# An attention and FFN kernel with its 483 work units queued in another order

## The chip, the cores and the metric

The kernel runs on one core of one Trainium2 chip. The metric is device time in microseconds (us), the median of several runs. A core has five engines that run side by side, each with its own in-order queue: TensorE (PE) multiplies matrices and reads its stationary operand in a separate weight load (PEld), VectorE (DVE) and ScalarE (ACT) work element by element and empty PSUM, the accumulator memory that only TensorE writes, GpSimd (POOL) does casts and small copies between SBUF tiles, and SyncE (SP) issues transfers, which 16 DMA engines carry out. An instruction waits at the head of its queue until the semaphores it needs have been counted up; everything behind it on that engine waits as well.

## The reference

The computation is an attention with a sparse mask, followed by a feed-forward block (FFN) whose hidden layer is the maximum of three products:

```python
scores = scale * np.matmul(q, k.transpose(0, 1, 3, 2))       # 4 batches, 8 heads, 768 rows, width 64
keep = is_global | is_local                                  # the first 8 keys, and the last 96
scores = np.where(keep, scores + bias, -1e9)                 # bias = -slope[head] * distance
a = np.exp(scores - max); a = a / (sum(a) + 1e-9)
x = np.matmul(a, v)                                          # brought to (3072, 512)
h = np.maximum(np.maximum(x @ w1, x @ w2), x @ w3)           # 512 -> 768
out = h @ w_out                                              # 768 -> 512
```

Inputs and output are float32. The kernel casts to bf16 on the chip.

## The kernel before

The 3072 rows are 24 tiles of 128 rows, six to a batch (tiles 0 to 5 are batch 0). For the FFN the tiles are gathered in seven chunks of 4, 2, 2, 4, 4, 4 and 4 tiles, so chunk 0 holds tiles 0 to 3, chunk 1 tiles 4 and 5, chunk 2 tiles 6 and 7, chunk 3 tiles 8 to 11, and so on. A tile needs keys of itself and of the tile before; the eight global keys are put over the first eight columns of a tile's transposed keys, where only later tiles read them.

The whole kernel is a list of units, written out by hand or by a planner as the string `SCHEDULE` (lines 25 to 57). The last lines of the kernel go through it in order, and each unit puts its instructions at the end of the queues of its engines. The scheduling is manual, so the order on every engine, SP's transfers among them, is the order of the string. The first letter names the unit, the numbers that follow its tile or part, and often as the last number the engine that does the copy (0 ACT, 1 DVE, 2 POOL, other values other ways):

- `l` (line 151) loads a part of q or k for a group of tiles: l0, l1, l2 are tiles 0 and 1, 2 and 3, 4 and 5 (q and k, 512 KB each), l3 is tiles 6 to 9 (four parts), l4 tiles 10 and 11. `c` (178) casts such a part to bf16, `x` (226) transposes it with eight matmuls into PSUM and copies the result out.
- `L` (160) loads q and k of one tile from tile 12 on, `C` with 0 (185) casts them, `X` (245) transposes them: with a last number 4 as one DMA transposition on SP, otherwise with eight matmuls and copies.
- `v` loads v of a tile (256 KB), `C` with 1 casts it. `V` and `G` copy the global rows and columns.
- `w` loads weights (w0.0 to w0.2 of 512 KB, w1.0 to w1.2 of 1024 KB), `W` casts a third of them: W0 serves the hidden blocks f = 0 and 1, W1 those of 2 and 3, W2 those of 4 and 5. `o` and `Q` do the same for the output weights. `K` and `B` make the masks.
- `S` (268) computes the scores of one tile and one half of the heads into PSUM (buffers sp0 or sp1) and takes the exponential on ACT. With a last number 1 the mask is added by two more matmuls, otherwise `M` (302) multiplies it on DVE.
- `A` (311) multiplies the probabilities with v into the same two PSUM buffers and normalises on DVE (rz, xb). `T` (335) transposes the result into `xT` of its chunk: by four matmuls and a copy, or with a last number 4 by one DMA transposition on SP.
- `F` (355) computes one of the three products of a chunk and hidden block: F0.4.1 is chunk 0, block 4, second product. ACT copies the first, DVE takes the maximum with the second and third. `O` (385) multiplies a tile's hidden layer with the output weights and stores it; `E` does so for the last chunk. `D` (432) is a few matmuls on zeros.

F, O, part of `x`, `X` and the first four `T` share three PSUM buffers, `psH`. The loads of q and k share five buffers, the loads of v six.

Of the kernel before, what the change touches and what calls it, by code (L numbers as in the profile page):

```python
# [22 lines left out]


SCHEDULE = """
    K0 K1 K2 K3 K4 K5 l1.0 l1.1 D0.3 c0.0.2 B0.1 B1.1 B2.1 B3.0 K6 B4.1 B5.1 c0.1.1 c1.0.2 x0.0.4 B6.1
    B7.1 x0.1.4 S0.0.1 v0 l2.0 l2.1 K7 S0.1.1 G0.0 S1.0.1 S1.1.0 x1.0.3 c1.1.2 M0.0 M0.1 M1.0 v1 x1.1.4
    C0.1.2 v2 A0.1 G1.2 S2.0.1 M1.1 c2.0.2 x2.0.1 C1.1.1 S2.1.0 G2.2 S3.0.1 M2.0 M2.1 C2.1.1 T0.1 S3.1.1
    M3.0 M3.1 c2.1.2 v3 A1.0 C3.1.0 w0.0 V1.2 x2.1.2 w1.0 A2.1 V2.2 A3.0 T1.0 T2.1 T3.1 W1.0.1 W0.0.0
    G3.2 S4.0.0 S4.1.0 F0.0.0 F0.1.0 M4.0 F0.2.0 F0.3.0 G4.1 S5.0.0 M4.1 S5.1.0 w0.1 W0.1.1 w0.2 W0.2.2  # L30
    V3.2 F0.0.1 F0.1.1 F0.0.2 F0.1.2 v4 C4.1.0 A4.0 V4.2 w1.1 W1.1.2 W2.0.0 F0.4.0 F0.5.0 M5.0 M5.1 w1.2
    W1.2.2 v5 W2.1.0 T4.0 F0.2.1 F0.3.1 l3.0 l3.2 F0.4.1 l3.1 c3.0.2 c3.2.2 F0.5.1 o2 C5.1.0 A5.1 l3.3
    F0.2.2 Q2.2 F0.3.2 W2.2.0 o0 T5.0 F0.4.2 o1 F0.5.2 x3.0.0 F1.0.0 F1.1.0 c3.1.1 F1.2.0 x3.2.0 Q0.2
    F1.0.1 F1.1.1 F1.2.1 l4.0 l4.1 c3.3.0 F1.0.2 F1.1.2 F1.2.2 x3.1.2 x3.3.1 F1.3.0 F1.4.0 Q1.2 F1.3.1
    S6.0.0 S6.1.0 v6 v7 v8 G6.0 F1.3.2 F1.5.0 v9 c4.0.1 F1.4.1 S7.0.0 S7.1.0 G7.2 v10 M6.0 M6.1 M7.0
    M7.1 O0.0.0 F1.4.2 c4.1.1 C6.1.2 C7.1.2 L12 F1.5.1 S8.0.0 S8.1.0 x4.0.0 O0.1.0 A6.0 x4.1.2 A7.1 V7.2
    F1.5.2 v11 T6.0 O0.2.0 T7.1 G8.2 C8.1.2 S9.0.0 S9.1.0 G9.1 v12 v13 O0.3.0 F2.0.0 F2.1.0 S10.0.0 M8.0
    M8.1 M9.0 M9.1 S10.1.0 C9.1.2 L13 L14 F2.0.1 F2.1.1 F2.0.2 A8.0 C12.0.1 F2.1.2 G10.2 O1.0.0 V8.2
    A9.1 X12.1 M10.0 M10.1 C10.1.0 C11.1.0 F2.2.0 S11.0.0 S11.1.0 M11.0 M11.1 L15 F2.3.0 F2.4.0 O1.1.0
    V9.2 A10.1 F2.2.1 V10.2 T8.0 F2.3.1 F2.5.0 T9.0 A11.1 F2.4.1 T10.0 F2.2.2 F2.3.2 T11.1 F2.4.2  # L40
    S12.0.0 S12.1.0 F2.5.1 C13.0.2 C14.0.2 C15.0.1 X13.4 F3.0.0 F3.1.0 F3.0.1 G12.1 C12.1.0 F3.2.0
    F3.1.1 F3.2.1 S13.0.0 S13.1.0 F2.5.2 v14 C13.1.0 C14.1.2 M12.0 M12.1 F3.0.2 F3.1.2 X14.4 F3.2.2
    X15.4 G13.2 M13.0 M13.1 S14.0.0 S14.1.0 F3.3.0 F3.4.0 F3.5.0 M14.0 M14.1 G14.1 A12.0 A13.1 F3.3.1
    F3.4.1 F3.5.1 S15.0.0 M15.0 S15.1.0 G15.0 v15 V13.2 L16 L17 v16 T12.4 v17 M15.1 O2.0.0 C15.1.0 A14.0
    V14.2 F3.3.2 F3.4.2 T13.4 F3.5.2 C16.1.0 C16.0.2 X16.3 T14.4 C17.0.2 A15.1 X17.4 O2.1.0 S16.0.0
    S16.1.0 G16.1 L18 V15.2 L19 T15.1 M16.0 O3.0.0 M16.1 F4.0.0 F4.1.0 F4.0.1 F4.1.1 C18.0.2 L20 C19.0.2
    A16.1 F4.2.0 F4.3.0 S17.0.0 S17.1.0 F4.2.1 F4.0.2 F4.3.1 v18 M17.0 v19 M17.1 X18.3 X19.4 C20.0.0
    V16.2 F4.1.2 C17.1.2 O3.1.1 A17.1 F4.2.2 F4.3.2 S18.0.0 M18.0 S18.1.0 M18.1 F4.4.0 T16.4 T17.4
    F4.4.1 C18.1.2 C19.1.1 F4.4.2 X20.4 G18.1 S19.0.0 S19.1.0 F4.5.0 L21 M19.0 M19.1 v20 F4.5.1 A18.0
    T18.4 F4.5.2 A19.1 T19.4 V19.1 C21.0.1 X21.4 G19.1 L22 C22.0.2 L23 X22.4 O3.2.1 O3.3.0 O4.0.1  # L50
    S20.0.0 S20.1.0 M20.0 G20.0 O4.1.0 F5.0.0 F5.1.0 F5.2.0 S21.0.0 S21.1.0 G21.2 F5.0.1 F5.1.1 M20.1
    M21.0 F5.3.0 F5.0.2 F5.1.2 F5.2.1 F5.2.2 v21 C20.1.1 C21.1.2 F5.4.0 S22.0.0 M21.1 S22.1.0 C23.0.0
    F5.3.1 M22.0 M22.1 F5.5.0 F5.3.2 A20.0 V20.2 G22.2 v22 F5.4.1 X23.4 v23 F5.5.1 T20.4 A21.1 V21.1
    T21.4 F5.4.2 F5.5.2 S23.0.0 S23.1.0 M23.0 O4.2.0 M23.1 C22.1.2 A22.0 C23.1.0 O4.3.0 V22.2 T22.4
    A23.1 T23.4 O5.0.1 O5.1.0 O5.2.1 O5.3.0 F6.0.0 F6.1.0 F6.0.1 F6.0.2 F6.2.0 F6.3.0 F6.4.0 F6.1.1
    F6.2.1 F6.1.2 F6.3.1 F6.4.1 F6.2.2 F6.3.2 F6.5.0 F6.4.2 F6.5.1 F6.5.2 E
"""


# [1 line left out]
def kernel(  # L61
# [272 lines left out]

    def u_XT(T, how):
        c, i = where[T]
        if i == 0:
            xT[c] = xT_pool.tile([128, NP, len(chunks[c]) * 128], BF16, name="xT", tag="xT")
        if how == 4:
            nc.sync.dma_start_transpose(out=xT[c][:, :, i * 128:(i + 1) * 128],  # L340
                                        in_=xb[T].rearrange("p h d -> p (h d)"))
            return
        if early(T):
            tp = psH.tile([128, NP, 128], BF16, name="xtp", tag="h")
        else:
            tp = psT.tile([128, NP, 128], BF16, name="xtp", tag="tp")
        x = xb[T].rearrange("p h d -> p (h d)")
        for jp in range(NP):
            nc.tensor.transpose(tp[:, jp], x[:, jp * 128:(jp + 1) * 128], identb)  # L349
# [4 lines left out]

    def u_F1(c, f, j):
        W = len(chunks[c]) * 128
        if f == 0 and j == 0:
            ht[c] = ht_pool.tile([128, NF, W], BF16, name="ht", tag="ht")
        ps = psH.tile([128, W], FP32, name="h", tag="h")
        for dm in range(4):  # L360
            nc.tensor.matmul(ps, w123[f // 2][:, dm, j, (f % 2) * 128:(f % 2) * 128 + 128],  # L361
                             xT[c][:, dm], start=(dm == 0), stop=(dm == 3))
# [147 lines left out]
```

## Time and profile before

| | |
|---|---|
| Median of 3 runs | 180.03 us (179.93 to 180.16) |
| Span of the profiled execution | 178.3 us |
| TensorE busy | 166.9 us, 94% |
| VectorE, ScalarE, GpSimd busy | 118.9, 103.1, 37.5 us |
| DMA moved | 35.52 MB, 83587 packets |
| DMA transpositions on SP | 11 of results (`xT<-xb`), 9 of q/k pairs (`qkT<-qkb`) |

The span is what the profiler saw from the first to the last instruction; the run time is a little longer. In the profile, a row of digits gives the busy share in 40 slices of the span (9 is 90% or more). The chain is the work that ended last, followed back step by step to what released each instruction. A row of a timeline gives start, duration, engine, line, operation, output and input, the number of instructions and, in brackets, how long the engine had been idle and what ended that. Matmul durations overlap, so what a unit costs TensorE is read from the distance of starts.

### The profile page before, as it was taken

The page shows a single profiled execution, that of the slowest core. Times are in us where ns is not written, and L with a number is a line of the kernel's source. Part 1 is how long each engine was busy: PE and PEld are TensorE (multiplying, and loading weights), DVE is VectorE, ACT ScalarE, POOL GpSimd, SP SyncE. Part 2 cuts the span into 40 slices and gives each one's busy share as a digit, 9 for nine tenths or more (in the row PEclk, how much of TensorE's full clock was granted, in tenths as well). Part 3 has the DMA queues.
Part 4 walks back from the last instruction along what each step waited for, and adds up shares of the span by engine and source line. Part 5 has one row for each costly group of instructions (what it writes and reads, how often), then busy time and mean ns, then how long its engine had stood idle before and what let it go on. Part 6 is the DMA issues. An engine that isn't in the chain of part 4 may idle for free.

```text
span 178.3 us, 3960 instructions
## 1 busy us (share of the span) xinstructions
PE 166.9 (94%) x1529; PEld 95.8 (54%) x1551; DVE 118.9 (67%) x237; ACT 103.1 (58%) x160; POOL 37.5 (21%) x65
## 2 busy tenths in 40 slices
PE   3599799999999999999999999999999999999992
...
DMA  5999999999998999989544999769889674610006
GB/s 140 292 271 242 357 320 384 320 361 358 251 193 213 229 254 236 174 171 233 94 90 118 159 247 235 157 132 186 173 153 294 136 143 146 224 42 4 0 11 226
DMA packets 83587, 35.52 MB, mean 199 GB/s; under 512 B 66160, under 2 KB 78320, under 8 KB 83568
## 3 DMA queue, kind: packets, MB, share of 16 engines
...
## 4 chain that ended last, share of the span: by engine, by line
PE 85%; DMA 8%; SPq 2%; issue 1%; POOL 1%; DVE 1%; ACT 1%; ACTq 0%
PE h L361 53%; PE po L376 17%; PE sp L283 6%; DMA rawv<-in_v_dram 4%; DMA rawp<-in_q_dram 4%; PE op L322 3%; PE op L325 2%; SPq L174 2%; PE tpp L239 2%; PE xtp L349 1%; SPq L158 1%; POOL qkp L183 1%; PE tp L261 1%; DVE xb L332 0%; ACT va L189 0%
## 5 line engine op out<-in xcount | busy, mean ns | idle before, releaser
L361 PE MATMUL h<-xT,w 128*128 128x512 bf16 (+1 forms) x491 | 99.2, 348 | 0.7 <-issue 0.2
L361 PEld LDWEIGHTS <-w 128*128 128x128 bf16 x504 | 46.9, 98 | 40.5 <-DVE w L427 0.3
L288 ACT ACTIVATE P<-sp 128x1024 bf16<-128x1024 f32 (+1 forms) x48 | 43.4, 955 | 20.6 <-PE sp L283 20.4
L368 DVE TENSOR_TENSOR h<-h,h 128x512 bf16<-128x512 bf16 (+1 forms) x42 | 25.3, 610 | 25.7 <-PE h L361 16.5
L366 ACT CAST h<-h 128x512 bf16<-128x512 f32 (+1 forms) x42 | 21.6, 533 | 21.5 <-PE h L361 21.3
L376 PE MATMUL po<-wo,ht 128*128 128x512 bf16 (+2 forms) x147 | 33.1, 362 | 0.5
L370 DVE TENSOR_TENSOR ht<-h,h 128x512 bf16<-128x512 bf16 (+1 forms) x42 | 25.1, 607 | 3.7 <-PE h L361 3.0
L307 DVE TENSOR_TENSOR P<-P,wmask 128x1024 bf16<-128x1024 bf16 x36 | 24.8, 718 | 3.6 <-ACT P L288 3.5
L376 PEld LDWEIGHTS <-ht 128*128 128x128 bf16 x156 | 14.0, 98 | 13.9
L382 ACT COPY ost<-po 128x512 f32<-128x512 f32 (+2 forms) x20 | 11.2, 564 | 17.8 <-PE po L376 17.7
L332 DVE TENSOR_TENSOR xb<-op,rz 128x512 bf16<-128x512 f32 x24 | 16.6, 692 | 0.8
L283 PEld LDWEIGHTS <-qkT 64*128 64x128 bf16 x352 | 10.2, 96 | 10.0 <-issue 8.0
L283 PE MATMUL sp<-qkT 64*128 64x128 bf16 x352 | 15.2, 223 | 0.4 <-DVE xb L332 0.4
L322 PEld LDWEIGHTS <-P 128*128 128x128 bf16 x192 | 12.5, 97 | 2.5 <-ACT P L288 0.2
L221 POOL COPY va<-vaf 8x260 int32<-8x260 int32 x14 | 6.3, 452 | 34.5 <-PE op L325 34.5
L198 POOL CAST qkb<-raw 128x1024 bf16<-128x1024 f32 x7 | 7.2, 1037 | 27.7 <-DMA raw<-in_q_dram 18.9
L322 PE MATMUL op<-va,P 128*128 128x65 bf16 x160 | 12.3, 193 | 0.7 <-ACT va L189 0.6
L239 PE MATMUL tpp<-identb,qkp 128*128 128x128 bf16 x96 | 8.5, 246 | 4.0 <-POOL qkp L183 3.4
L325 PEld LDWEIGHTS <-P 128*128 128x128 bf16 x160 | 10.4, 97 | 2.2 <-issue 0.7
L239 PEld LDWEIGHTS <-qkp 128*128 128x128 bf16 x96 | 7.0, 111 | 5.8 <-POOL qkp L183 4.3
L325 PE MATMUL op<-va,P 128*128 128x65 bf16 x128 | 9.9, 193 | 0.0
L243 ACT COPY qkT<-tpp 128x1024 bf16<-128x1024 bf16 (+1 forms) x9 | 7.9, 874 | 3.4 <-PE tpp L239 3.4
...
## 6 DMA issues: line engine op xcount, KB each, us to landing
...
```

What stands on the lines that cost most here:

```text
L239: nc.tensor.transpose(tp[:, e, j - lo], qb["p", n, s][:, e, 2 * j:2 * j + 2].rearrange("i h d -> i (h d)"), identb)
L283: nc.tensor.matmul(sp[:, hh, j2, ds], qT(T - ds, 1)[hsl, jp], qT(T, 0)[hsl, jp], start=not how, stop=True, skip_group_check=True)
L288: nc.scalar.activation(P[:, :, 0:n], sp.rearrange("p a b d n -> p (a b) d n")[:, :, 0:n], AF.Exp, bias=0.0, scale=scale)
L307: nc.vector.tensor_mul(P, P, wmask[:, g, :, 0:2])
L322: nc.tensor.matmul(o, P[:, i, 0], heads(va[T])[:, h], start=True, stop=(t == 0), skip_group_check=True)
L325: nc.tensor.matmul(o, P[:, i, 1], heads(va[T - 1])[:, h], start=False, stop=True, skip_group_check=True)
L332: nc.vector.tensor_tensor(out=x.rearrange("p (g h) d -> p g h d", g=2), in0=o4[:, :, :, 0:64], in1=rz[:, :, :, None].to_broadcast([128, 2, ...
L361: nc.tensor.matmul(ps, w123[f // 2][:, dm, j, (f % 2) * 128:(f % 2) * 128 + 128], xT[c][:, dm], start=(dm == 0), stop=(dm == 3))
L366: nc.scalar.copy(h01, ps)
L368: nc.vector.tensor_max(h01s[c, f], h01s[c, f], ps)
L370: nc.vector.tensor_max(ht[c][:, f], h01s[c, f], ps)
L376: nc.tensor.matmul(po, ht[c][:, f, tt * 128:(tt + 1) * 128], wo[:, f, cols], start=(f == 0), stop=(f == NF - 1))
```

## The change

The same 483 units stand in another order. The order alone moves three kinds of things:

- The attention of tiles 0 to 5 up to its scores stands ahead of the first FFN unit, with `A4`, `T4`, `A5` and `T5` between the first FFN units of chunk 0; in the order before, S4 stands ahead of the first FFN unit and S5 behind it. In the opening, part x3.0 of tiles 6 to 9 also comes ahead of the FFN, the four l3 loads stand among the weight loads instead of behind them, and `D0.3` stands behind x0.0 instead of first. From there on, FFN units of chunks 0, 1 and 2 are interleaved more finely.
- X16 and X18 go from matmuls to a DMA transposition (11 by DMA instead of 9), and T8, T9 and T10 as well (14 by DMA instead of 11).
- Seventy-odd units have another engine for their copy, cast or PSUM buffer. On the whole POOL gets casts of w and v from ACT and DVE. Six score units have their mask from matmuls, as before, but partly others (S1.1, S4.0, S4.1, S5.1 in the place of S1.0, S2.0, S3.0, S3.1).

Two lines of code allow for an order in which the first unit of a chunk is not always the same: the tile is made by whichever unit comes first. The diff, with the string cut to what is spoken of:

```diff
-    K0 K1 K2 K3 K4 K5 l1.0 l1.1 D0.3 c0.0.2 B0.1 B1.1 B2.1 B3.0 K6 B4.1 B5.1 c0.1.1 c1.0.2 x0.0.4 B6.1
-    B7.1 x0.1.4 S0.0.1 v0 l2.0 l2.1 K7 S0.1.1 G0.0 S1.0.1 S1.1.0 x1.0.3 c1.1.2 M0.0 M0.1 M1.0 v1 x1.1.4
-    C0.1.2 v2 A0.1 G1.2 S2.0.1 M1.1 c2.0.2 x2.0.1 C1.1.1 S2.1.0 G2.2 S3.0.1 M2.0 M2.1 C2.1.1 T0.1 S3.1.1
-    M3.0 M3.1 c2.1.2 v3 A1.0 C3.1.0 w0.0 V1.2 x2.1.2 w1.0 A2.1 V2.2 A3.0 T1.0 T2.1 T3.1 W1.0.1 W0.0.0
-    G3.2 S4.0.0 S4.1.0 F0.0.0 F0.1.0 M4.0 F0.2.0 F0.3.0 G4.1 S5.0.0 M4.1 S5.1.0 w0.1 W0.1.1 w0.2 W0.2.2
-    V3.2 F0.0.1 F0.1.1 F0.0.2 F0.1.2 v4 C4.1.0 A4.0 V4.2 w1.1 W1.1.2 W2.0.0 F0.4.0 F0.5.0 M5.0 M5.1 w1.2
-    W1.2.2 v5 W2.1.0 T4.0 F0.2.1 F0.3.1 l3.0 l3.2 F0.4.1 l3.1 c3.0.2 c3.2.2 F0.5.1 o2 C5.1.0 A5.1 l3.3
-    F0.2.2 Q2.2 F0.3.2 W2.2.0 o0 T5.0 F0.4.2 o1 F0.5.2 x3.0.0 F1.0.0 F1.1.0 c3.1.1 F1.2.0 x3.2.0 Q0.2
-    F1.0.1 F1.1.1 F1.2.1 l4.0 l4.1 c3.3.0 F1.0.2 F1.1.2 F1.2.2 x3.1.2 x3.3.1 F1.3.0 F1.4.0 Q1.2 F1.3.1
-    S6.0.0 S6.1.0 v6 v7 v8 G6.0 F1.3.2 F1.5.0 v9 c4.0.1 F1.4.1 S7.0.0 S7.1.0 G7.2 v10 M6.0 M6.1 M7.0
-    M7.1 O0.0.0 F1.4.2 c4.1.1 C6.1.2 C7.1.2 L12 F1.5.1 S8.0.0 S8.1.0 x4.0.0 O0.1.0 A6.0 x4.1.2 A7.1 V7.2
...
-    A9.1 X12.1 M10.0 M10.1 C10.1.0 C11.1.0 F2.2.0 S11.0.0 S11.1.0 M11.0 M11.1 L15 F2.3.0 F2.4.0 O1.1.0
-    V9.2 A10.1 F2.2.1 V10.2 T8.0 F2.3.1 F2.5.0 T9.0 A11.1 F2.4.1 T10.0 F2.2.2 F2.3.2 T11.1 F2.4.2
...
+    K2 B3.1 c0.1.1 K7 B4.1 B1.2 B7.2 c0.0.0 K0 K6 K3 B0.1 B2.1 B6.1 x0.0.4 D0.3 x0.1.4 K4 B5.1 K5
+    l1.0 c1.0.2 l1.1 v1 c1.1.2 K1 S0.0.1 S1.1.1 M1.1 S1.0.0 C1.1.2 G0.2 G1.2 x1.0.3 M0.0 x1.1.4 M1.0
+    S0.1.1 S2.0.0 S2.1.0 v0 C0.1.1 A1.0 l2.1 c2.1.2 V1.0 G2.2 l2.0 c2.0.2 M2.1 M2.0 S3.0.0 S3.1.0
+    l3.0 x2.1.1 M3.1 T1.0 x2.0.2 G3.1 M0.1 A0.0 S4.1.1 v2 v3 M3.0 C2.1.2 c3.0.2 A2.0 V2.0 x3.0.2
+    C3.1.2 A3.1 S4.0.1 G4.1 M4.0 T2.1 T0.0 w0.0 W0.0.2 T3.1 S5.1.1 S5.0.0 M5.0 v4 v5 w0.1 F0.1.0
+    l3.3 V3.2 F0.0.0 M4.1 C4.1.2 A4.1 V4.0 c3.3.0 W0.1.2 C5.1.2 F0.1.1 F0.0.1 w0.2 W0.2.2 w1.0 M5.1
+    A5.1 T4.1 x3.3.2 F0.1.2 W2.0.2 T5.0 F0.0.2 F1.1.0 F1.1.1 F1.1.2 W1.0.1 l3.1 l3.2 F0.5.0 c3.2.1
+    c3.1.2 x3.1.2 F0.3.0 x3.2.4 F0.2.0 G6.0 S7.1.0 S7.0.0 F1.2.0 w1.1 W1.1.1 F0.3.1 W2.1.2 F0.5.1
+    S6.0.0 S6.1.0 M6.1 F1.2.1 F0.2.1 w1.2 W1.2.2 v7 G7.0 S8.1.0 l4.1 c4.1.2 S8.0.0 M7.0 F0.3.2 M6.0
+    F0.2.2 M7.1 F0.4.0 F1.4.0 v6 C6.1.2 F1.2.2 W2.2.2 A6.1 C7.1.2 G8.2 F1.5.0 x4.1.0 F0.5.2 A7.0 L12
+    o2 Q2.2 F1.3.0 l4.0 o0 o1 v8 v9 Q0.2 T6.1 M8.0 v12 F1.5.1 F1.5.2 c4.0.0 S9.0.0 S9.1.0 G9.0
+    F1.3.1 F1.3.2 F1.4.1 T7.1 L13 v10 C12.0.3 F0.4.1 F2.2.0 M9.1 V7.2 x4.0.0 C9.1.1 F1.0.0 F2.2.1
+    F0.4.2 S10.1.0 L15 L14 S10.0.0 G10.0 X12.1 Q1.2 O0.3.1 O0.2.0 v13 M10.1 M8.1 O0.0.0 M9.0 F1.4.2
+    v14 C8.1.2 A8.0 V8.2 v11 C10.1.2 M10.0 F2.4.0 F1.0.1 F1.0.2 S11.0.0 S11.1.0 O0.1.0 A9.0 V9.2
+    T8.4 C13.0.2 X13.4 F2.5.0 M11.0 F2.4.1 C15.0.2 F2.4.2 S12.0.0 S12.1.0 T9.4 F2.5.1 F2.5.2 M12.0
+    A10.0 F2.3.0 T10.4 C14.0.2 M11.1 V10.2 F2.0.0 X14.4 F2.2.2 C11.1.1 L16 X15.4 v16 C13.1.1 O1.0.1
+    F2.3.1 A11.0 O1.1.0 M12.1 F2.0.1 G12.0 F2.1.0 F2.1.1 T11.1 S13.0.0 L19 v15 L18 S13.1.0 F2.0.2
+    G13.1 F2.3.2 M13.0 F2.1.2 F3.2.0 S14.0.0 S14.1.0 L17 F3.4.0 F3.4.1 O2.1.1 C12.1.2 A12.0 T12.4
+    F3.4.2 F3.3.0 M14.1 F3.0.0 F3.0.1 C14.1.0 M13.1 G14.1 F3.5.0 C19.0.0 M14.0 F3.2.1 A13.1 V13.2
+    F3.2.2 C16.0.2 X16.4 T13.4 F3.5.1 S15.0.0 M15.0 C18.0.0 S15.1.0 C15.1.2 F3.5.2 M15.1 X19.4
...
+    A16.1 L21 L20 v19 F4.4.1 S19.0.0 v23 v20 L22 v21 S18.1.0 F4.5.1 F4.3.0 S17.1.0 S18.0.0 M19.0
...
+    A23.1 F5.5.0 F5.5.1 F5.5.2 T23.4 O5.2.1 O5.3.1 F6.0.0 F6.0.1 F6.3.0 F6.4.0 F6.5.0 F6.4.1 F6.5.1
+    F6.4.2 F6.1.0 O5.1.0 F6.0.2 F6.3.1 F6.2.0 F6.1.1 F6.2.1 O5.0.0 F6.2.2 F6.3.2 F6.1.2 F6.5.2 E
```

```diff
     def u_XT(T, how):
         c, i = where[T]
-        if i == 0:
+        if c not in xT:
             xT[c] = xT_pool.tile([128, NP, len(chunks[c]) * 128], BF16, name="xT", tag="xT")
...
     def u_F1(c, f, j):
         W = len(chunks[c]) * 128
-        if f == 0 and j == 0:
+        if c not in ht:
             ht[c] = ht_pool.tile([128, NF, W], BF16, name="ht", tag="ht")
```

More of the change, by code (lines that the diff above doesn't have):

```diff
@@ L36 @@
-    M7.1 O0.0.0 F1.4.2 c4.1.1 C6.1.2 C7.1.2 L12 F1.5.1 S8.0.0 S8.1.0 x4.0.0 O0.1.0 A6.0 x4.1.2 A7.1 V7.2
-    F1.5.2 v11 T6.0 O0.2.0 T7.1 G8.2 C8.1.2 S9.0.0 S9.1.0 G9.1 v12 v13 O0.3.0 F2.0.0 F2.1.0 S10.0.0 M8.0
-    M8.1 M9.0 M9.1 S10.1.0 C9.1.2 L13 L14 F2.0.1 F2.1.1 F2.0.2 A8.0 C12.0.1 F2.1.2 G10.2 O1.0.0 V8.2
-    A9.1 X12.1 M10.0 M10.1 C10.1.0 C11.1.0 F2.2.0 S11.0.0 S11.1.0 M11.0 M11.1 L15 F2.3.0 F2.4.0 O1.1.0
-    V9.2 A10.1 F2.2.1 V10.2 T8.0 F2.3.1 F2.5.0 T9.0 A11.1 F2.4.1 T10.0 F2.2.2 F2.3.2 T11.1 F2.4.2
@@ L41 @@
[L41 to L55, printed above, removed]
@@ L56 @@
-    F6.2.1 F6.1.2 F6.3.1 F6.4.1 F6.2.2 F6.3.2 F6.5.0 F6.4.2 F6.5.1 F6.5.2 E
+    K2 B3.1 c0.1.1 K7 B4.1 B1.2 B7.2 c0.0.0 K0 K6 K3 B0.1 B2.1 B6.1 x0.0.4 D0.3 x0.1.4 K4 B5.1 K5
[3 more added lines that the diff above has]
+    C3.1.2 A3.1 S4.0.1 G4.1 M4.0 T2.1 T0.0 w0.0 W0.0.2 T3.1 S5.1.1 S5.0.0 M5.0 v4 v5 w0.1 F0.1.0
@@ new lines @@
+    F2.3.1 A11.0 O1.1.0 M12.1 F2.0.1 G12.0 F2.1.0 F2.1.1 T11.1 S13.0.0 L19 v15 L18 S13.1.0 F2.0.2
+    G13.1 F2.3.2 M13.0 F2.1.2 F3.2.0 S14.0.0 S14.1.0 L17 F3.4.0 F3.4.1 O2.1.1 C12.1.2 A12.0 T12.4
+    F3.4.2 F3.3.0 M14.1 F3.0.0 F3.0.1 C14.1.0 M13.1 G14.1 F3.5.0 C19.0.0 M14.0 F3.2.1 A13.1 V13.2
+    F3.2.2 C16.0.2 X16.4 T13.4 F3.5.1 S15.0.0 M15.0 C18.0.0 S15.1.0 C15.1.2 F3.5.2 M15.1 X19.4
+    F3.0.2 A14.0 T14.4 O2.0.1 X18.4 v18 V14.0 A15.1 F3.1.0 F3.3.1 V15.1 F3.3.2 F3.1.1 T15.0 F3.1.2
+    C17.0.2 X17.4 G15.2 S16.0.0 S16.1.0 F4.1.0 F4.4.0 M16.0 G16.2 M16.1 v17 C16.1.2 F4.5.0 C17.1.2
```

7 lines of the change are left out of this document (added).

## The prediction

> **What bounds the kernel now.** First the busy shares and the chain of what ended last: TensorE is busy 94% of a 178.3 us span, and 85% of the chain is TensorE's own work.
>
> ```profile
> PE 166.9 (94%) x1529; PEld 95.8 (54%) x1551; DVE 118.9 (67%) x237; ACT 103.1 (58%) x160; POOL 37.5 (21%) x65
> PE   3599799999999999999999999999999999999992
> DMA  5999999999998999989544999769889674610006
> ```
>
> In the slices TensorE has gaps only in the first 24 us, and the DMA engines are full for the first 55 us or so. Then the chain in order of time, around the start of the first FFN block (line 361) and where a transposition stands between FFN matmuls.
>
> ```profile
> 13.07 7.08 DMA rawv<-in_v_dram
> 20.18 0.63 ACT va L189
> ...
> 22.52 0.40 PE xtp L349 x4
> 22.92 0.55 PE sp L283 x16
> 23.48 0.34 PE h L361
> ...
> 39.10 0.39 PE xtp L349 x4
> 39.49 1.73 PE h L361 x8
> 41.22 0.45 PE tpp L239 x8
> ```
>
> Until 20.2 us the chain waits for v of tile 3. From 23.5 us it is TensorE alone. I make that exact with prices of whole units, each read from such pieces: a q/k part `x` or pair `X` of eight transpositions 0.447 us, a result `T` of four 0.224, one score group `S` 0.277 (first tile of a batch 0.165), a pair of bias matmuls 0.454 (0.23), an `A` 0.485 (0.26), an FFN unit `F` 0.864 (0.436 for a chunk of two tiles), an `O` 1.30, the warm-up 0.65. All units of the kernel come to 160.3 us. What precedes T5's transposition is 0.65 + 6 `x` 2.68 + `S` 3.10 + bias 2.27 + `A` 2.69 + 5 `T` 1.12 + 16 `F` 13.82 = 26.3 us, and it starts at 39.10: 12.8 us have been lost by then. Nearly nothing is lost later, except about 0.1 us at each tile's pair of `S`, which both orders pay. So the time is work plus what the opening loses.
>
> Last, POOL's rows in the opening.
>
> ```profile
> 36.77 1.04 POOL L183 CAST qkp<-rawp 128x1024 bf16<-128x1024 f32 x1 [1.58 <-DMA rawp<-in_q_dram]
> 38.28 1.04 POOL L183 CAST qkp<-rawp 128x1024 bf16<-128x1024 f32 x1 [0.46 <-DMA rawp<-in_k_dram]
> ```
>
> The second starts when load l3.2 lands, at 38.2 us. With full DMA engines this is a clock for bytes: ahead of it and with it SP has issued six parts of 512 KB, six v of 256 KB, w0.x at 3 x 512 KB, w1.x at 3 x 1024 KB and two l3 parts, 10,240 KB in all.
>
> **Transposition by DMA: the gain.** X16 and X18 (8 each) and T8, T9, T10 (4 each) leave TensorE: 2 x 0.447 + 3 x 0.224 = 1.57 us, and as TensorE is full there, all of it counts. Their seven PSUM copies go too (ACT 586 ns, DVE about 420); nothing waits for those. In their place stand five more steps on SP, 1.22 to 1.26 us each by the median of the 20 there now, with landing 2.4 (`T`) and 3.2 us (`X`) after the start of the issue. SP takes O0.1's store at about 67 us, then T8, X13, T9, T10, X14: five at 1.25 with a wait for POOL's cast of tile 13 and for tile 10's result, so X14 is issued near 72 and lands near 76. S14 comes up on TensorE near 79, F3.2.0, which needs T8 to T10, near 78. Margin 2 to 3 us: cost zero, and without that cover microsecond for microsecond. The loads L16, L19, L18, L17 behind them feed S16 and later, some 20 us on. The rest of SP's queue is in order with room.
>
> The Trainium skill speaks against this part: "VectorE: DVE Perf Modes", section "Rules for kernel authors", says to transpose 128x128 on TensorE where a PSUM destination will do and by DMA otherwise, and the section on the three transpose paths has 390 ns against 1309. By that rule the five moves would be a loss (the slower rival below); the trace here has 0.056 us of a full TensorE per block against a queue with slack, so I go by the rows.
>
> **The opening: the cost.** Ahead of F0.1.0 there is now also S5, and four l3 parts are loaded ahead of the late weights. Two floors:
>
> (1) *Bytes.* Ahead of w1.1, and with it, SP now issues six q/k parts, six v, four l3 parts, w0.0 to w0.2, w1.0: again exactly 10,240 KB. So w1.1 lands at 38.2, its cast (W1.1.1, DVE 693 ns) ends at about 39.0, and F0.3.1 can't start before. Work ahead of F0.3.1 in the new order: 0.65 + 10 `x` 4.47 + `S` 3.65 + bias 2.27 + `A` 2.69 + 6 `T` 1.34 + 9 large and 4 small `F` 9.52 = 24.6. Lost: 39.0 - 24.6 = 14.4 us. The other weights by the same clock set lower floors (w0.2 13.5, w1.2 13.6).
>
> (2) *ScalarE.* Between the copy of x0.1 (9.3) and the copy of T0 that F0.1.0 needs, ACT has three masks 1.25, two short exps 1.2, eight long at a pitch of about 0.95, 7.6, the copies x1.1, x2.0, x3.0, T1, T0 3.4 and V1, V2 0.8: 14.2 us, so 23.5 at the least. Scores and results share two PSUM buffers, so it waits as well: an `A` holds its buffer for 0.5 us, then rz, xb 1.1, then the next S and exp. Stepping through: exp of S0.0 at 11.0, of S2.0 at 15.2, A1 at 16.2, S3's exps end 20.3, x2.0 is copied at 21.7, S4.1's exp ends 23.3, x3.0 is copied 24.6, S4.0's exp ends 25.9, T0 is copied 26.4. F0.1.0 at 26.4 against 11.8 of work: lost 14.6. If the matmuls are at full rate from 9.5 on, each step comes earlier and F0.1.0 starts at 25.4: lost 13.6.
>
> The floors agree; I take 14.4, bounds 13.6 (loads land 1.3 us earlier, full rate early) and 16 (some fifteen hand-overs of that chain each 0.1 late). Against 12.8 the opening costs +1.6 (+0.8 to +3.2).
>
> On the clock: the eight transpositions at 12.20 still start 107 ns apart and those at 15.00 at 56, so before was at half rate until about 13.5 us; the warm-up matmuls now stand between x0.0 and x0.1 and TensorE has no gap from 6.05 to 9.5. "TensorE: Matmul & The Clock Gate" of the Trainium skill, Part 1, gives full rate after about 3.4 us of sustained work; by it the second walk (13.6) is the likelier, by the row of before, where 5.8 us from 7.70 were needed, the first.
>
> **Casts and copies that change engine.** POOL gets w and v casts (about 1.04 and 0.61 us), ACT loses them. After 24 us TensorE waits for neither, so relief there is worth nothing. POOL in the opening ends W0.1 near 27.6 and W0.2 near 30.4, before F0.1.1 and F0.1.2 ask (28.6 and 31). One v cast on POOL took 1073 ns instead of 610 beside DVE's masks: some 0.4 us where it recurs, behind slack.
>
> **New waits after the opening.** The three `psH` buffers turn over faster than 2.6 us in places (F1.3.2, F1.4.1 near 52 have 0.1 us of margin). Bounds 0 (before shows none) and 1.0 (five of 0.2, the size of a late copy); I take 0.2, nearer to before.
>
> **Sum.** -1.57 + 1.6 + 0.2 = +0.2 on the profiled 178.3: 178.5. The runs' median of 180.03 is 1.7 above that span, so 180.3.
>
> **Rivals.**
> - *Slower: SP's queue between 66 and 73 us becomes the bound.* Five transpositions in a row behind a store, with the DMA rings still behind with loads. For: the longest of those now took 2.32 us to issue and 4.5 to land. Against: the medians. With the longest, X14 lands 5 x 1.07 later, about 81.5; S14 waits 2.5 us; the time is 182.8; half of it 181.5. It decides from X14 landing later than 79. Chance 0.28, with other late inputs of that size.
> - *Faster: the opening is no worse than 13.6.* Before, v of tile 3 landed 2.6 us after that of tile 2, where 256 KB otherwise take 1.1 to 1.2; without such a lag w1.1 lands near 36.9 and the second walk decides. 178.3 - 1.57 + 0.8 + 0.1 = 177.6, so 179.3. Chance 0.25.
> - *The order does nothing:* S4 stands ahead of F0 already and A4, A5 still come between FFN units, so the opening stays at 12.8: -1.57, 178.5. Against: both floors. Chance 0.04.
>
> **Chances and range.** The forecast has 0.43 (own range 179.7 to 181.0). Measurements tell about 0.2% (0.36 us) from no change: the forecast is inside that for 0.25, slower for 0.18. With the rivals: faster 0.29, same 0.25, slower 0.46. Range 179.0 to 182.2.
>
> **What would show it.** F0.1.0 at 25.4 to 26.5 us, with ACT's copy of T0 as its releaser; DVE's cast of w1.1 at about 38.2 and F0.3.1 right behind; no other gap on TensorE; X14 landed by 77. Wrong if F0.3.1 runs before 38, if `tpp` or `sp` of later tiles wait for DMA, or if TensorE shows gaps at the `psH` turns.

## The result, and the profile after

The changed kernel takes 185.71 us (median of 4 runs, 184.44 to 187.85) against 180.07 us (179.93 to 180.16). It is slower by a factor of 1.0289, 95% interval [1.0254, 1.0324]. The forecast of 180.3 us, and its range to 182.2, missed it by 5.4 and 3.5 us. Ratios and their intervals leave out disturbed runs, such as the one at 187.85; medians and ranges hold all runs.

The page of the changed kernel, first its busy times, then the rows of TensorE and of its granted clock in 40 slices, the chain by engine, and the group of DVE's masks (`M`):

```profile
PE 167.5 (91%) x1502; PEld 96.1 (52%) x1523; DVE 123.9 (67%) x236; ACT 95.9 (52%) x150; POOL 46.6 (25%) x72
...
PE   0685899999999995999999999999999999999993
...
PEclk9999699999999999799999999999999999999999
...
PE 86%; DVE 8%; DMA 2%; issue 1%; ACT 1%; ACTq 0%
...
L308 DVE TENSOR_TENSOR P<-P,wmask 128x1024 bf16<-128x1024 bf16 x36 | 29.2, 824 | 7.6 <-ACT P L289 7.6
```

The same group in the kernel before:

```profile
L307 DVE TENSOR_TENSOR P<-P,wmask 128x1024 bf16<-128x1024 bf16 x36 | 24.8, 718 | 3.6 <-ACT P L288 3.5
```

TensorE is as busy as before (167.5 against 166.9 us) although it shows 27 matmuls fewer. DVE has 5 us more, 4.4 of it in the same 36 masks: a mask's mean is 824 ns, and was 718. There are two dents: one in the opening, and one in the sixteenth slice of TensorE (about 69 to 73.5 us) with a drop of the granted clock right behind it. Before had a smaller dent in the opening and none later.

As in the prediction, I take the start of a unit on TensorE less the work queued ahead of it as the time lost so far. Lines of the changed kernel are those of before plus one.

| lost, us, by the start of | F0.1.0 | F0.3.1 | S9 | S12 | S14 | F6.0.0 |
|---|---|---|---|---|---|---|
| before | 12.7 | 12.8 | 13.2 | 13.5 | 13.7 | 14.6 |
| changed | 15.3 | 16.2 | 16.5 | 16.8 | 21.0 | 21.9 |

The difference is 3.3 us by the end of the opening, stays there to S12 (69.1 us), grows by 4.0 from S12 to S14 (84.1 us) and then stays again. With 1.57 us less work that is 3.3 + 4.0 - 1.57 = 5.7 us, and the spans differ by 183.9 - 178.3 = 5.6.

The second place, in the timeline of the changed kernel (start, duration, engine, line, operation; in brackets the idle time ahead and its releaser):

```profile
68.18 0.69 DVE L333 TENSOR_TENSOR xb<-op,rz 128x512 bf16<-128x512 f32 x1
68.28 3.00 POOL L199 CAST qkb<-raw 128x1024 bf16<-128x1024 f32 x3
...
68.79 3.04 DVE L308 TENSOR_TENSOR P<-P,wmask 128x1024 bf16<-128x1024 bf16 x1
...
71.75 0.41 DVE L369 TENSOR_TENSOR h<-h,h 128x256 bf16<-128x256 bf16 x1
72.21 0.60 PE L362 MATMUL h<-xT,w 128*128 128x256 bf16 x4 [2.13 <-DVE h L369]
```

DVE's mask M11.0, 0.69 us elsewhere, takes 3.04. (By the order on DVE it is M11.0, which stands right ahead of the maximum of F2.4.1; the expectations below call the same instruction M11.1, which comes later, at 74.64 us, and takes 0.68.) It begins half a microsecond after POOL has begun three casts in a row (tiles 13, 15, 14) and ends half a microsecond after the last. The maximum behind it on DVE, that of F2.4.1, is late by as much, the `psH` buffer that it would free is late, and F2.5.2 waits 2.13 us. Behind that gap, twelve matmuls of 128x256 take 2.75 us instead of 1.47; the granted clock over stretches shows it, and shows the opening (columns: stretch and its length, TensorE busy with its count, granted clock, DMA share, GB/s). First the changed kernel:

```profile
12.00:18.00 6.00, 3.15 (x65) 1.00 1.19 295
18.00:24.00 6.00, 5.32 (x75) 0.72 1.15 231
...
68.00:78.00 10.00, 7.81 (x72) 0.83 0.87 195
```

The same stretches of the kernel before:

```profile
12.00:18.00 6.00, 5.63 (x72) 1.00 1.28 253
18.00:24.00 6.00, 4.67 (x95) 1.00 1.08 359
...
68.00:78.00 10.00, 9.89 (x109) 1.00 0.93 194
```

The pattern of the mask is in the opening too: casts of the changed kernel that DVE does while POOL does one.

```profile
14.65 1.29 DVE L190 CAST vaf<-rawv 128x512 bf16<-128x512 f32 x1
...
39.12 1.04 POOL L428 CAST w<-wst 128x1024 bf16<-128x1024 f32 x1 [3.14 <-DMA wst<-in_moe_w_dram]
39.20 1.50 DVE L428 CAST w<-wst 128x1024 bf16<-128x1024 f32 x1
...
40.76 0.60 PE L362 MATMUL h<-xT,w 128*128 128x512 bf16 x2 [0.24 <-DVE w L428]
```

The v cast takes 0.42 us elsewhere, that of w1.1 0.69. The second releases F0.3.1. With three casts on ScalarE (the first experiment) DVE comes first at this place, and then it is POOL's cast that takes longer:

```profile
39.01 0.69 DVE L428 CAST w<-wst 128x1024 bf16<-128x1024 f32 x1
...
39.04 1.56 POOL L428 CAST w<-wst 128x1024 bf16<-128x1024 f32 x1 [3.14 <-DMA wst<-in_moe_w_dram]
```

### The profile page after: what moved, and what is told of

Its sections match the earlier page's. It is cut to its first block, busy times and chain, and to the rows that moved or that the text cites. A ratio compares the mean times of both kernels' runs of the same rounds, so it can differ in the third digit from the quotient of the medians.

```text
span 183.9 us, 3904 instructions
## 1 busy us (share of the span) xinstructions
PE 167.5 (91%) x1502; PEld 96.1 (52%) x1523; DVE 123.9 (67%) x236; ACT 95.9 (52%) x150; POOL 46.6 (25%) x72
## 4 chain that ended last, share of the span: by engine, by line
PE 86%; DVE 8%; DMA 2%; issue 1%; ACT 1%; ACTq 0%
PE h L362 50%; PE po L377 17%; PE sp L284 6%; PE tpp L240 3%; PE op L323 3%; PE op L326 3%; DVE P L308 2%; DMA rawp<-in_q_dram 2%; DVE qkT L244 2%; PE sp L276 1%; PE xtp L350 1%; DVE xb L333 1%; DVE w L428 1%; PE wp L437 1%; DVE vaf L190 1%
## 5 line engine op out<-in xcount | busy, mean ns | idle before, releaser
L362 PE MATMUL h<-xT,w 128*128 128x512 bf16 (+1 forms) x487 | 101.6, 351 | 3.3 <-DVE h L369 2.1
L369 DVE TENSOR_TENSOR h<-h,h 128x512 bf16<-128x512 bf16 (+1 forms) x42 | 25.4, 608 | 15.7 <-PE h L362 12.7
L308 DVE TENSOR_TENSOR P<-P,wmask 128x1024 bf16<-128x1024 bf16 x36 | 29.2, 824 | 7.6 <-ACT P L289 7.6
L371 DVE TENSOR_TENSOR ht<-h,h 128x512 bf16<-128x512 bf16 (+1 forms) x42 | 25.4, 607 | 9.4 <-PE h L362 8.2
L377 PEld LDWEIGHTS <-ht 128*128 128x128 bf16 x156 | 14.5, 98 | 15.3 <-DVE ht L371 0.4
L383 ACT COPY ost<-po 128x512 f32<-128x512 f32 (+2 forms) x17 | 9.4, 558 | 22.2 <-PE po L377 22.1
L190 POOL CAST va<-rawv 128x512 bf16<-128x512 f32 x15 | 10.2, 686 | 21.0 <-DMA rawv<-in_v_dram 18.4
L323 PEld LDWEIGHTS <-P 128*128 128x128 bf16 x192 | 13.0, 100 | 3.4 <-PE sp L284 0.8
L323 PE MATMUL op<-va,P 128*128 128x65 bf16 x160 | 12.8, 194 | 1.3 <-DVE xb L333 0.6
L222 POOL COPY va<-vaf 8x260 int32<-8x260 int32 x8 | 3.4, 430 | 37.5 <-PE op L326 37.3
L383 DVE COPY ost<-po 128x512 f32<-128x512 f32 (+1 forms) x9 | 5.8, 646 | 10.4 <-PE po L377 10.3
L326 PEld LDWEIGHTS <-P 128*128 128x128 bf16 x160 | 10.7, 98 | 2.3 <-issue 0.6
```

The lines of the kernel that those rows point to most:

```text
L308: nc.vector.tensor_mul(P, P, wmask[:, g, :, 0:2])
L323: nc.tensor.matmul(o, P[:, i, 0], heads(va[T])[:, h], start=True, stop=(t == 0), skip_group_check=True)
L326: nc.tensor.matmul(o, P[:, i, 1], heads(va[T - 1])[:, h], start=False, stop=True, skip_group_check=True)
L377: nc.tensor.matmul(po, ht[c][:, f, tt * 128:(tt + 1) * 128], wo[:, f, cols], start=(f == 0), stop=(f == NF - 1))
```

## The experiments

Theory A: a POOL instruction keeps DVE's masks and casts out while it runs, a row of them for the whole row; the new order puts such rows beside DVE's work that TensorE soon needs. Rivals: the turnover of `psH` (B), the DMA transpositions, ScalarE, and TensorE's clock.

**Three casts to ScalarE**, no POOL row beside M11.0:

```diff
-    T8.4 C13.0.2 X13.4 F2.5.0 M11.0 F2.4.1 C15.0.2 ... T10.4 C14.0.2 M11.1
+    T8.4 C13.0.0 X13.4 F2.5.0 M11.0 F2.4.1 C15.0.0 ... T10.4 C14.0.0 M11.1
```

> The changed kernel with the three casts of q/k pairs 13, 14, 15 on ScalarE instead of GpSimd. Theory A (GpSimd's three casts in a row keep VectorE's mask multiplication M11.1 out of SBUF for 2.4 us; TensorE then runs dry for 2.1 us, falls to half rate and loses another 1.6 us): M11.1 takes about 0.69 us again, TensorE has no gap at 70 us and no half-rate stretch after it; 3.4 to 3.9 us less, about 182 us. Theory B (the three psH buffers turn over too fast in this order, whoever casts): the gap near 70 us stays, 185 to 186 us. Theory C (the DMA transpositions at 71 to 78 us hold something up): the gap stays too.

183.43 us (182.29 to 184.05), 1.0184 [1.0137, 1.023]. In its timeline:

```profile
68.80 0.68 DVE L308 TENSOR_TENSOR P<-P,wmask 128x1024 bf16<-128x1024 bf16 x1
```

The mask is back at its usual length and F2.5.2 starts at 69.96 with 16.9 us lost (19.1 in the changed kernel). 2.3 us are won, against the 3.4 to 3.9 that I had expected. Between S12 and S14 1.2 us are still lost, where before lost 0.2: A10 now loses 0.6 waiting for ScalarE, which has the casts, and S14 0.5, of which the trace gives 0.34 to X14's landing.

**The row broken**: a copy of eight elements on POOL that reads the result of the cast ahead of it, so that POOL waits for itself.

```diff
+    def u_Z(T):
+        nc.gpsimd.tensor_copy(brk, qb[T][0:1, 0, 0:8])
-    T8.4 C13.0.2 X13.4 ... C15.0.2 F2.4.2
+    T8.4 C13.0.2 Z13 X13.4 ... C15.0.2 Z15 F2.4.2
```

> The changed kernel with a tiny copy on GpSimd behind the casts of 13 and 15 that reads what the cast has just written, so that GpSimd waits for its own cast before it goes on. Nothing else moves. Theory A in its narrow form (the mask is kept out because the casts follow each other without a gap): M11.1 gets in after the first cast, ends near 69.9 instead of 71.8, takes 1.1 to 1.3 us, and 2.5 to 3.9 us are won. Theory A in its broad form (any GpSimd work keeps VectorE out until GpSimd runs dry): M11.1 still takes 3 us. Theories B and C: the same time as the changed kernel.

185.03 us, but from 181.98 to 187.11; the ratio, 1.0152 [1.0101, 1.0202], rests on 181.98 and 183.47 alone. So the times settle little here, and the profile, of the 181.98, has to. Its timeline, POOL and then DVE and TensorE:

```profile
67.65 1.03 POOL L199 CAST qkb<-raw 128x1024 bf16<-128x1024 f32 x1
68.75 0.53 POOL L443 COPY brk<-qkb 1x8 bf16<-1x8 bf16 x1
69.23 1.03 POOL L199 CAST qkb<-raw 128x1024 bf16<-128x1024 f32 x1
...
68.16 1.07 DVE L308 TENSOR_TENSOR P<-P,wmask 128x1024 bf16<-128x1024 bf16 x1
...
69.61 0.60 PE L362 MATMUL h<-xT,w 128*128 128x256 bf16 x4 [0.17 <-DVE h L369]
```

The same three casts stand on the same engine at the same place, with work added, and the mask takes 1.07 us. It gets in as soon as POOL pauses: POOL's little copy is now the one that waits, 0.53 us instead of the 0.18 of the next. By F6.0.0 18.0 us are lost, 3.9 fewer than in the changed kernel; 0.6 of that is luck in the opening. What the row had cost is the difference in growth of the lost time from S12 to S14: 4.15 against 0.91, 3.2 us.

**The gap filled**: ten matmuls on zeros ahead of F2.5.2, so that TensorE waits as long without being idle.

```diff
+        yp = psT.tile([128, 512], FP32, name="yp", tag="tp")
+        for _ in range(n):
+            nc.tensor.matmul(yp, zeros[:, 0:128], zeros, start=True, stop=True)
-    T9.4 F2.5.1 F2.5.2
+    T9.4 F2.5.1 Y10 F2.5.2
```

> The changed kernel with ten matmuls on zeros (2.16 us, into the psT buffer) ahead of F2.5.2, where TensorE runs dry for 2.1 us. The mask still waits. Theory A1 (the half-rate stretch after the gap comes from the gap): the 128x256 matmuls after it start 109 ns apart instead of 213, and about 1.6 us are won: 184 us. Theory A2 (the rate falls for another reason, such as the load so far): the half-rate stretch stays, and the time is that of the changed kernel, 185 to 186 us.

185.15 us (184.25 to 186.86), 1.0298 [1.0237, 1.0359]. In its trace, the stretch of the gap and the filler:

```profile
68.00:78.00 10.00, 9.54 (x106) 1.00 0.76 171
```

```profile
70.77 2.32 PE L443 MATMUL yp<-zeros 128*128 128x512 bf16 x10
73.06 0.60 PE L362 MATMUL h<-xT,w 128*128 128x256 bf16 x4
73.98 1.47 PE L362 MATMUL h<-xT,w 128*128 128x256 bf16 x12
```

The clock stays at 1.00 (0.83 without filler) and the twelve matmuls take 1.47 us again: the half rate came with the gap and is gone without it. Its price is the growth from F2.5.2 to S14: 1.85 us in the changed kernel, 0.84 here, so 1.0 us, less than I had thought. The time didn't follow (the two ranges overlap), as the profiled run lost 1.3 us at F2.2.1 (57.6 us), where the changed kernel's profile had lost under 0.1: there a cast of DVE had met two of POOL's.

```profile
54.22 0.41 DVE L369 TENSOR_TENSOR h<-h,h 128x256 bf16<-128x256 bf16 x1
...
54.89 2.10 DVE L196 CAST qkb<-raw 128x512 bf16<-128x512 f32 x1
...
55.11 1.03 POOL L431 CAST wo<-wost 128x1024 bf16<-128x1024 f32 x1
56.09 0.61 POOL L190 CAST va<-rawv 128x512 bf16<-128x512 f32 x1
```

POOL runs without a pause from 54.20 to 56.70. The maximum, which reads one operand from PSUM, takes its usual 0.41 us within the row; the cast from SBUF to SBUF, 0.42 elsewhere, takes 2.10 and ends 0.3 after it.

**Two casts in the row instead of three**: the cast of tile 13 is put ahead of M10.0.

> The changed kernel with the cast of q/k block 13 (POOL, 128x1024) put earlier in POOL's queue, ahead of the mask of tile 10, so that two casts in a row (blocks 15 and 14) stand beside the mask M11.1 in place of three. Theory A (POOL's row of casts keeps DVE's mask out until the whole row is done): M11.1 takes about 2.0 us (3.04 in the changed kernel, 0.69 undisturbed), TensorE's wait ahead of F2.5.2 falls from 2.1 to about 1.1 us, no half-rate matmuls follow it, and the time falls by 1.0 to 2.6 us, to 183.1 to 184.7. Rival A' (the lock is given back after each POOL instruction, and the 3.04 us had another cause): M11.1 takes 0.7 to 1.7 us. Rival B (the psH buffers): no change, 185.7.

184.43 us (183.5 to 186.52), 1.0225 [1.0197, 1.0252]. Timeline:

```profile
68.78 2.02 POOL L199 CAST qkb<-raw 128x1024 bf16<-128x1024 f32 x2
...
69.28 2.06 DVE L308 TENSOR_TENSOR P<-P,wmask 128x1024 bf16<-128x1024 bf16 x1
...
71.73 0.60 PE L362 MATMUL h<-xT,w 128*128 128x256 bf16 x4 [1.15 <-DVE h L369]
```

One cast fewer, and the mask is shorter by 0.98 us, TensorE's wait by 0.98 us. Both numbers are as expected. With the runs before, A holds at this place against B and against a lock that is given back after each instruction: DVE is kept out for the whole row. (The moved cast meets the mask ahead, M10.0, which takes 1.70 us at 65.54.)

That a whole row always keeps DVE out is not shown. In the changed kernel's own profile a mask gets in between two casts that follow each other, and the second of them waits:

```profile
47.59 1.03 POOL L428 CAST w<-wst 128x1024 bf16<-128x1024 f32 x1
48.58 1.07 POOL L190 CAST va<-rawv 128x512 bf16<-128x512 f32 x1
...
47.69 1.48 DVE L308 TENSOR_TENSOR P<-P,wmask 128x1024 bf16<-128x1024 bf16 x1
```

The mask takes 1.48 us, one cast and its own length, and the v cast 1.07 instead of 0.61. At 20.40 us it is the same (0.93 and 1.07). What decides between the two kinds of meeting these runs don't show.

**DMA transpositions in the order before**: X16, X18, T8 and T9 go to SP there, 24 transpositions.

```diff
-    X16.3 ... X18.3 ... T8.0 ... T9.0
+    X16.4 ... X18.4 ... T8.4 ... T9.4
```

> The kernel before, with X16, X18, T8 and T9 by DMA transposition and nothing else. By the price of the forecast (0.447 us for a pair, 0.224 for a result) it is 1.34 us faster: 178.7 us. If SP's queue or the DMA engines can't hide them there, TensorE shows waits at S16, S18 or F3.0.0, and it is the same as before or slower.

182.21 us (181.9 to 183.1), 1.0131 [1.0103, 1.016]. The first case of my expectation was wrong by 3.5 us; the second came, with waits at the three places that it names: F3.0.0, S16 and, 0.34 us only, S18. The larger two:

```profile
76.97 1.24 PE L361 MATMUL h<-xT,w 128*128 128x512 bf16 x5 [1.79 <-DMA xT<-xb]
...
100.62 0.62 PE L283 MATMUL sp<-qkT 64*128 64x128 bf16 x16 [1.24 <-DMA qkT<-qkb]
```

In that order the results are asked for soon after they are ready, and the transfer has no slack. The gain of a transposition taken off TensorE was real only where its consumer was far.

**The transpositions of the new order undone**, on top of the three casts on ScalarE:

```diff
-    T8.4 ... T9.4 ... T10.4 ... X16.4 ... X18.4
+    T8.0 ... T9.0 ... T10.0 ... X16.3 ... X18.3
```

> The kernel with three casts on ScalarE (183.43 us), and with the result transposes of tiles 8, 9, 10 and the q/k pairs 16 and 18 put back on TensorE, with an eviction on ScalarE or DVE each: 28 transposes at 0.056 us. If the transposes taken off TensorE are a gain of their full length in this order, 183.4 + 1.57 = 185.0 us. If they filled time in which TensorE waited anyway, 183.4. If the DMA transposes hold work up here as they did in the kernel before (there they cost 2.2 us), 181 to 182.5.

186.7 us (186.4 to 188.6), 1.039 [1.0338, 1.0442], so 3.3 us slower than with them: 1.57 us of work, and 1.4 more lost by F6.0.0 in waits for POOL's cast of tile 16, for DVE's xb and for ScalarE. That is more than any case of the expectation. In the new order the moves are worth at least what was forecast.

**Three pieces of the opening taken off DVE**, on top of the three casts:

```diff
-    C0.1.1 ... G3.1 ... W1.1.1
+    C0.1.2 ... G3.0 ... W1.1.2
```

> The kernel with three casts on ScalarE (183.43 us), and with three pieces of the opening taken off DVE: the cast of v block 0 (1.29 us instead of 0.42 beside a POOL cast) and the cast of w1.1 (1.50 instead of 0.69) go to POOL, the copy of the kept keys of tile 3 (0.58 instead of 0.17) to ScalarE. Theory A (DVE held out by POOL is a part of the opening's loss): F0.1.0 starts 0.5 to 1.0 us earlier than 26.9, F0.3.1 at 39.5 to 40.2 in place of 40.8, and the time falls by 0.6 to 1.5 us, to 182 to 182.8. Rival (ScalarE's walk and the landings alone set the opening, as the forecast had it): no change within 0.3, 183.4; slower if POOL's longer casts (1.07 against 0.61) are late in their turn.

183.76 us (182.7 to 184.8): no gain. In the profiled run F0.1.0 starts at 25.70 (26.80 without the edit), with TensorE at full rate all along; but then F0.5.0 and x3.1 wait for POOL's casts of a weight and of l3.1, whose loads had not landed earlier, and further on masks meet other casts (one at 45.14 us takes 1.54 us, one at 53.49 the same), and F1.2.2 and F1.3.2 wait for DVE:

```profile
49.07 0.60 PE L362 MATMUL h<-xT,w 128*128 128x256 bf16 x4 [1.14 <-DVE ht L371]
...
55.41 1.12 PE L362 MATMUL h<-xT,w 128*128 128x256 bf16 x8 [0.63 <-DVE h L369]
```

With the opening 1 us earlier, other masks meet other casts.

**The warm-up matmuls first**, on top of the three casts (`D0.3` ahead of `K2`):

> The kernel with three casts on ScalarE (183.43 us), and with the dummy matmuls at the head of TensorE's queue, where the kernel before has them, in place of behind the first transposes. If the clock in the opening is a part of its loss, TensorE's first half-rate stretch ends some 3 to 5 us earlier and F0.1.0 starts 0.3 to 1.0 us earlier, and the time falls by as much, to 182.4 to 183.1. If not (the evictions and casts set the opening, and TensorE only waits for them): 183.4 within 0.3.

184.04 us (183.81 to 184.44), no gain: F0.1.0 at 27.52, and the granted clock from 18 to 24 us at 0.54, lower than without the edit (0.79). Three matmuls on zeros at 1.2 us did not keep it up over the gaps at 12 to 18 us.

**The opening's gaps filled**, on top of the broken row, with 3, 4 and 6 matmuls on zeros, and with 29 in all:

```diff
-    S0.1.1 S2.0.0 ... A1.0 ... S3.0.0
+    S0.1.1 D0.3 S2.0.0 ... D0.4 A1.0 ... D0.6 S3.0.0
```

> The kernel with POOL's row of casts broken (one profiled run 181.98 us, four runs 182.0 to 187.1), and with 3, 4 and 6 matmuls on zeros ahead of S2.0.0, A1.0 and S3.0.0, where TensorE waited 0.8, 0.6 and 1.3 us in the opening. Theory C (TensorE's gaps between 12 and 18 us let its clock fall, 0.72 of full rate granted from 18 to 24 us, and that makes the new opening late and the runs unequal): the granted clock from 18 to 24 us is 0.95 or more, F0.1.0 starts near 25.7 to 26.2 in place of 26.9, the mean clock of all runs is near 1.00, and the time is 181.0 to 182.5 with a spread under 1.5 us. Rival (ScalarE, DVE and the landings set the opening and TensorE's rate is hidden behind them): F0.1.0 within 0.3 of 26.9, 182 to 184; if the zeros are in the way, later.

> The same with more zeros: 3, 6, 6, 10 and 4 matmuls ahead of S1.0.0, S2.0.0, A1.0, S3.0.0 and A2.0, so that TensorE has no gap from 9 us on; a part of them stands in the way of work (at full rate 29 cost 6.3 us of TensorE, its gaps there are about 4). Theory C: the granted clock is 1.00 throughout and the runs agree within 1 us, at a time 0 to 2 us above the kernel with fewer zeros. Rival: the clock still falls in some runs, the spread stays over 2 us.

185.86 us (185.43 to 186.41) and 189.72 us (187.55 to 190.4), 1.0328 [1.0308, 1.0348] and 1.05 [1.0438, 1.0562]. The clock did what it was to do, 1.00 from 12 to 24 us in both profiles, and it didn't help. With 13 matmuls A2 starts at 22.65 us, where the broken row alone has 22.27 at a granted clock of 0.72, and A2 waits for DVE's xb in both: TensorE's rate there is hidden behind DVE and ScalarE. So the theory of the clock (C in these two expectations) falls for the opening's time, though the zeros also take TensorE's time, so the test is not a clean one. For the spread of the runs it came true once (1.0 us with 13 matmuls) and once not (2.9 us with 29). Then this, in the timeline of the first, DVE and POOL:

```profile
25.32 2.72 DVE L217 COPY qkT<-kg 128x32 bf16<-128x32 bf16 x1
...
24.87 0.61 POOL L190 CAST va<-rawv 128x512 bf16<-128x512 f32 x1
25.43 1.03 POOL L428 CAST w<-wst 128x1024 bf16<-128x1024 f32 x1
26.41 0.61 POOL L190 CAST va<-rawv 128x512 bf16<-128x512 f32 x1
26.97 1.03 POOL L428 CAST w<-wst 128x1024 bf16<-128x1024 f32 x1
```

A copy of 32 columns, 0.17 us elsewhere, waits through four casts that end at 28.00, and ends at 28.04. S5 waits 1.41 us for it. With 29 matmuls on zeros the same copy takes 2.72 us again, in the broken row's profile, where it met two casts, 1.08, and in the changed kernel's 0.19: there the second of the four casts, W0.1, waited for its load until 26.99.

**POOL's later casts made short**, on top of the three casts: v from tile 6 on, the last w3 piece and the w_out pieces are cast in 2 of every 64 columns; three memsets on DVE stand ahead of F0.3.1.

```diff
+    def thin(out, in_):
+        nc.gpsimd.tensor_copy(out[:, :, 0:64:32], in_[:, :, 0:64:32])
```

> The kernel with three casts on ScalarE (183.43 us), and with POOL's casts from 46 us on made short: v from tile 6 on, the last w3 piece and three of the w_out pieces are cast in 2 of every 64 columns only (the rest of these tiles holds stale or constant values, set once by three DVE memsets ahead of F0.3.1, so the output isn't the reference's); every wait and every order stays. Theory A (after the opening, what is left of the loss is DVE held out by POOL's casts): TensorE's waits at F2.2.1 (56.8 us, 0.9), at A10 (71, 0.6) and at S14 (81, 0.6) go, start minus work ahead grows from 43 us to the end by about 2.2 (0.1 for each S pair, as in the kernel before) in place of 3.8, and the time falls by 1.0 to 1.7 us, to 181.7 to 182.4. Rival (the psH buffers, the DMA transposes or ScalarE's three casts make these waits): 183.4 within 0.4.

182.93 us (182.82 to 183.23), 1.0161 [1.0144, 1.0178]: 0.5 us less, half of the least that was expected, and inside the spread of the kernel with whole casts. The wait at F2.2.1 went. That at A10 stayed:

```profile
70.63 0.20 PE L330 MATMUL op<-va,P 128*128 128x65 bf16 x1 [0.41 <-ACT P L296]
```

It is ScalarE's, which the rival had said, and my memsets cost 0.6 us at F0.2.1. What is plainer is the spread: four runs within 0.4 us, where the same kernel with whole casts has 1.8 and the broken row 5. That fits runs that differ by which casts meet which DVE work, but doesn't show it: the kernel with the warm-up first has whole casts and a spread of 0.6 us.

**All POOL casts followed by such a copy**, in the changed kernel:

> The changed kernel with a copy of 8 elements on POOL behind each POOL cast, which reads the cast's result, so that POOL waits for its own cast and no two casts run back to back. Theory A (only a row of POOL casts keeps DVE out for long; between two casts that wait for each other DVE gets in): no DVE operation takes more than about 1.1 us longer than undisturbed, M11.1 takes 0.7 to 1.7 us in place of 3.04, TensorE's wait at F2.5.2 falls from 2.1 to 0.6 or less, and the time falls from 185.7 to 182 to 184. Rival A' (each cast locks by itself, rows don't matter): the sum of DVE's lost time is the same, 185 or more. If POOL's 0.2 to 0.6 us for each copy makes its casts late where TensorE waits for them (in the opening above all), 186 and more.

183.9 us (182.85 to 186.17), 1.019 [1.0135, 1.0245]. M11.0 takes 1.07 us and F2.5.2 loses 0.3, as A has it. In the profiled run, 186.17, the slowest of the four, F0.1.0 starts at 29.12; the copies load POOL there, but the granted clock is 0.50 as well from 18 to 24 us, and which of the two made it late this one profile doesn't show. Of all these kernels none comes near 180 us.

## Why the prediction was wrong

**The failed step** is "Casts and copies that change engine", in its last sentence: "One v cast on POOL took 1073 ns instead of 610 beside DVE's masks: some 0.4 us where it recurs, behind slack." I had read the row as a POOL cast that is slowed and priced POOL's side alone, and put DVE's side at nothing. Who comes first holds the other off: DVE's mask is the one that waits when POOL is already running, and at M11.0 it waited for as long as POOL's row went on. That one row, unbroken, cost 3.2 us (changed kernel against broken row): 2.1 us of waiting, and most of the rest half rate behind it (1.0 us by the filled gap). Nor was there slack: M11.0 stands on DVE ahead of the maximum that frees F2.5.2's buffer. What there was to see it by: masks that operate on SBUF alone, and in the new order three `C` with a last 2 and no wait between them. (By the two strings 88 units change engine or buffer, more than the seventy-odd named above.) And the profile of before has DVE's side too. Three of its masks take 1.03, 0.90 and 1.10 us instead of 0.68, each behind a POOL cast that had begun; the second stands behind the very v cast of 1073 ns. The first:

```profile
32.11 1.03 POOL L427 CAST w<-wst 128x1024 bf16<-128x1024 f32 x1
...
32.66 1.03 DVE L307 TENSOR_TENSOR P<-P,wmask 128x1024 bf16<-128x1024 bf16 x1
```

Before also has C13 and C14 on POOL back to back, 70.82 to 72.84 us (the new order adds C15 as a third, which DVE had); DVE has xb and two maxima there, all with an operand in PSUM, and none is longer than usual.

The sum adds up so: of the 5.4 us by which the time lies above the forecast, 3.8 are growth from S12 to S14 beyond the 0.2 that was taken, and 1.7 the opening beyond its 1.6.

The Trainium skill has this lock: "SBUF — State Buffer", section "Who interferes with whom", says that a VectorE instruction with two SBUF inputs contends with a GpSimd instruction that reads SBUF, calls the shared ports an exclusive lock, and of VectorE's two-port modes says that whoever issues first has them for its whole instruction while the other is blocked fully. The mask and the casts are such a pair, the maximum with its PSUM operand is none, and the runs agree on both; they differ on the length at M11.0, where the mask took 3.04, 2.06 and 1.07 us beside three casts, two, and a row broken after the first, so there a whole row and not one instruction.

**The opening, +1.6 forecast, +3.3 measured.** The bounds held it nearly (+0.8 to +3.2), the value taken didn't. F0.1.0 was to start at 26.4 by the cold walk or 25.4 by the warm; it started at 27.11, and between 25.70 and 27.52 in eight of the other kernels of this order (not in those with breaks or fillers in the opening). It came right behind S5's scores, not released by ScalarE's copy of T0. F0.3.1 was to start at 39.0 and did at 40.76. The floor of bytes did not set that, although w1.1 landed at 39.07 instead of 38.2: DVE was copying x3.2 until 39.29, and then the cast took 1.50 instead of 0.69 beside POOL's cast of W2.1. In the broken row's profile w1.1 had landed 1.9 us earlier (POOL's W2.1 starts on it at 37.22), and still F0.3.1 came at 40.14, without a wait, against 40.04 with three casts on ScalarE, where it waits for nothing either. At S9 these two have 2.6 and 2.7 us lost over before. So about 0.7 of the 3.3 is the lock and its luck. Of the rest 2.4 and 2.5 us are lost by F0.1.0 already, where the cold walk had 1.9: hand-overs of that walk that I had set too short. Which of them, no run singles out. The clock alone wasn't it, by the filled opening; the one early start, 25.70, had three pieces off DVE and the full rate at once.

**The transpositions, -1.57.** Right in size by TensorE's work at the forecast's prices (158.7 against 160.3 us), and undoing them cost 3.3. That they are free was right here and would have been wrong in the order before, where 24 of them made it 2.2 us slower. I had argued it from margins of 2 to 3 us at S14 and F3.2.0. In the changed kernel nothing on TensorE waits for them, but the stall had made part of that margin (see SP's queue below).

**New waits, +0.2 (bounds 0 and 1.0).** Measured 4.0 us from S12 to S14; with the row broken 0.7 more than before, inside the bounds. By mechanism `psH` turned over late, the third of the forecast's signs of being wrong, but because of DVE's wait.

**The rivals.** SP's queue: X14 landed at 81.3, far behind the 79 from which it was to decide. S14 stood only at 84.1 because of the stall, so it cost nothing there; with the stall removed by the three casts on ScalarE it cost some of 0.5 us, and with the row broken nothing. The full-rate walk came in one profile (25.70) and brought no gain, since landings and masks held up what followed. The time lay beyond every case I had: all of them moved one transfer or one walk, none an engine that holds another off.
